# The spectrum of step one stored with the frequency outside: another word order between two stages of a long convolution

## The chip, the cores and the metric

The kernel runs on one core of a Trainium2 chip. The metric is the device time of one execution in microseconds (us). Of the core's engines, TensorE multiplies matrices out of the on-chip memory SBUF into the accumulator memory PSUM, ScalarE and VectorE work on both memories, GpSimd works on SBUF, and SyncE here only issues the transfers. Each engine takes its instructions in program order and waits for the others through semaphores.

## What is computed

The input x has 2048 tokens by 640 channels. A first block gates x with a long convolution, a second one mixes the tokens with an MLP. Shift, scale and gate of both come from c and w_mod.

```python
def _A_ref(q, k, v, shift_k, ssm_k, ssm_D):
    ...                                    # k_shift: causal convolution of k with 4 taps
    kv = k_shift * v
    kv_f = rfft(kv padded to 4096 tokens)
    kf_f = rfft(ssm_k padded to 4096)
    y = irfft(kv_f * kf_f)[:2048] + kv * ssm_D
    return q * y

def _B_ref(x, w1, b1, w2, b2):
    h = _layernorm(x)
    u = _gelu(einsum("bsd,sf->bdf", h, w1) + b1)
    return transpose(einsum("bdf,fs->bds", u, w2) + b2)

h = _layernorm(x) * (1 + ca) + sa
x = x + ga * _A_ref(h, A_k, A_v, A_shift_k, A_ssm_k, A_ssm_D)
h = _layernorm(x) * (1 + cb) + sb
x = x + gb * _B_ref(h, B_w1, B_b1, B_w2, B_b2)
```

The change lies in the Fourier transform of kv and of the convolution kernel (`ssm_k`). The names of the transforms are shortened here; the lines are otherwise those of the reference.

## The kernel before

The 640 channels are taken in five passes of 128 channels (`c` = 0 to 4, loop at line 510); a pass holds its channels as two halves of 64, one on the SBUF partitions 0 to 63 and one on 64 to 127. The 2048 tokens are split into 64 by 32, and the transform is done in two steps of matrix products.

**Step one** (`step1(side, t)`, line 210) is the transform over the 64. `side` 0 is the data kv (tile `x`, named X), `side` 1 the convolution kernel (tile `p`, named KSP), and `t` takes 8 of the 32 channels of each half. For each such channel `a` one operand column block is the stationary operand (64 columns; from X it steps by 32 words, from KSP it is unbroken), and the constant F1 (128 columns: half `h`, then frequency `k1`) is the moving one. Real and imaginary part (`ri`) go to the partitions 0 to 63 and 64 to 127 of one PSUM tile of 1024 words. Then ScalarE copies the tile into `T_z` (view `Z`, line 220). Eight such tiles fill the 8192 words of `T_z` for a pass.

**Step two** (`f2(g)`, line 224) is the transform over the 32, for 8 frequencies `k1` at a time. For each `k1`, part `ri` and half `h` there is one matmul: the stationary operand is a constant of 64 columns (`W2`), the moving operand 64 words of `T_z`, namely both sides and the 32 channels of half `h` at frequency `k1`. So it needs all eight tiles of step one. ScalarE then copies the kernel's spectrum out (`kt`, line 238), VectorE multiplies (tile `p`), and GpSimd, for the last block VectorE, adds the products into `Y`.

**The way back** is `i2` (line 255), whose result goes to the second half of `T_z` as `T2` (line 271), and `i1` (line 273); `gate` and `spill` finish a pass.

The order is written out by hand (`manual_schedule`). After f2 of a pass come step one's tiles 0 and 1 of the next pass's data, ScalarE's permutation of the next kernel (`perm`, line 164), `i2` and `i1` with data tiles 2 and 3 in between, and the four kernel-side tiles. Of these, tile 0 has its matmuls ahead of the second half of `i1` and its copy after it (`later=True`, run as `k0()`), because the copy overwrites T2. In pass 0 the order differs: step one stands at the start (lines 486 and 491), the four data tiles of pass 1 come straight after f2, and the four kernel tiles after `i1`. PSUM has three tiles in a ring for all of these and a fourth of its own. VectorE runs the products of kv (`kv_ops`) for a later pass between its f2 instructions. The modulation (`mod_load`, `mod_part`, line 342) runs within pass 0. After the five passes comes the token MLP (lines 432, 951 and 1026).

Of the kernel before, what the change touches and what calls it, by code (L numbers as in the profile page):

```python
# [11 lines left out]
AF = mybir.ActivationFunctionType  # L12
# [37 lines left out]
def mixer_kernel(ctx: ExitStack, tc: tile.TileContext, q, k, v, shift_k, ssm_k, ssm_D, w1, b1, w2, b2, c,  # L50
# [7 lines left out]
    act, dve, pool, pe, sync = nc.scalar, nc.vector, nc.gpsimd, nc.tensor, nc.sync  # L58
# [3 lines left out]
    def mem(tag, n, name=None):  # L62

        return sb.tile([128, n], F32, name=name or tag, tag=tag, bufs=1)
# [4 lines left out]
    def psum(slot=None):  # L69

        uid[0] += 1
        slot = ring[uid[0] % len(ring)] if slot is None else slot
        return psp.tile([128, 1024], F32, name=f"pst_{uid[0]}", tag=f"pst{slot}", bufs=1)
# [6 lines left out]
    T_z, T_y, T_v1 = mem("z", 8192), mem("y", 4096), mem("v", 4520)  # L80
# [11 lines left out]
    KT = [T_kt[:, 512 * i:512 * i + 512] for i in range(2)]  # L92
    TV = T_kt[:, 1024:1536].rearrange("p (n i) -> p n i", i=64)

    Z = T_z.rearrange("p (s t a k e) -> p s t a k e", s=2, t=4, a=8, e=2)
    T2 = T_z[:, 4096:8192].rearrange("p (a m e) -> p a m e", a=32, e=2)
    Y = T_y.rearrange("p (r i k) -> p r i k", r=2, i=32)
    W2 = [t.rearrange("p (k m) -> p k m", m=64) for t in T_w2]
# [111 lines left out]
    def step1(side, t, later=False):  # L210

        ps = psum()
        for a in range(8):
            i = 8 * t + a
            lhs = KSP[:, i] if side else X.rearrange("p (m i) -> p i m", i=32)[:, i]
            o = 512 * (a % 2) + 128 * (a // 2)
            for ri in range(2):
                pe.matmul(ps[64 * ri:64 * ri + 64, o:o + 128], lhs, F1[:, 128 * ri:128 * ri + 128], start=True,  # L218
                          stop=True)
        evac = lambda: act.activation(Z[:, side, t].rearrange("p a k e -> p e a k"),  # L220
                                      ps.rearrange("p (e a k) -> p e a k", a=8, e=2), AF.Copy)
        return evac if later else evac()

    def f2(g):

        ps = psum()
        for kk in range(8):
            k1 = 8 * g + kk
            for ri in range(2):
                for h in range(2):  # L230
                    o = 128 * kk + 64 * ri
                    rhs = bass.AP(tensor=T_z.tensor, offset=T_z.offset + 128 * h + 2 * k1,
                                  ap=[T_z.ap[0], [256, 32], [1, 2]])
                    pe.matmul(ps[64 * h:64 * h + 64, o:o + 64], W2[k1 // 32][:, 2 * (k1 % 32) + ri], rhs, start=True, stop=True)  # L234
        pv = ps.rearrange("p (m s i) -> p m s i", s=2, i=32)
        xs_ = pv[:, :, 0]
        kt = KT[g % 2]
        act.activation(kt.rearrange("p (m i) -> p m i", i=32), pv[:, :, 1], AF.Copy)  # L238
        pa, pb = P[:, 1024 * (g % 2):1024 * (g % 2) + 512], P[:, 1024 * (g % 2) + 512:1024 * (g % 2) + 1024]
        m16 = lambda t: t.rearrange("p (m i) -> p m i", i=32)  # L240

        def mul():
            TT(dve, m16(pa), xs_, m16(kt), ALU.mult)
            sw = bass.AP(tensor=kt.tensor, offset=kt.offset + 32, ap=[kt.ap[0], [64, 8], [-32, 2], [1, 32]])
            TT(dve, pb.rearrange("p (k r i) -> p k r i", k=8, r=2), xs_.rearrange("p (k r) i -> p k r i", r=2), sw,
               ALU.mult)

        def add(eng=pool):
            for ri, t, op in ((0, pa, ALU.subtract), (1, pb, ALU.add)):
                t = t.rearrange("p (k r i) -> p r i k", k=8, r=2)  # L250
                TT(eng, Y[:, ri, :, 8 * g:8 * g + 8], t[:, 0], t[:, 1], op)
        return mul, add
# [20 lines left out]
    def i1(half, slot=None):  # L273

        ps = psum(slot)
        for jj in range(8):
            for ri in range(2):
                for e in range(2):
                    p = slice(64 * e, 64 * e + 64)
                    for b in range(2):  # L280
                        n2 = 16 * b + 8 * half + jj
                        pe.matmul(ps[64 * b:64 * b + 64, 512 * e + 64 * jj:512 * e + 64 * jj + 64],  # L282
                                  V1[p, ri, n2], T2[p, :, 32 * ri + n2], start=ri == 0, stop=ri == 1)
        return ps
# [200 lines left out]
    for t in range(4):  # L485
        step1(0, t)
# [3 lines left out]
    for t in range(4):  # L490
        step1(1, t)
# [18 lines left out]
    for c in range(NC):  # L510
# [36 lines left out]
        if c == 0:  # L547
            mod_load(0, 4, P[:, 0:1920])
            for t in range(4):
                step1(0, t)  # L550
            ps = psum()
# [45 lines left out]
        else:  # L597
# [6 lines left out]
            t = mem("in", 4288, "wb3")  # L604
# [4 lines left out]
        if c:  # L609
            dv(7 if cn is not None else 8)  # L610
            i2(0)
            if cn is None:
                mod_part(tap, 3, pl[3])
                i2(1, dve)
                t = mem("y", 4096, "wb2")
# [19 lines left out]
        for half in range(2):  # L635
            ps = i1(half)
# [122 lines left out]
    ps = i1(1, s1)  # L759
# [121 lines left out]
    for f_ in range(4, NF):  # L881
        ps = psum().rearrange("p (h m) -> p h m", h=2)
# [202 lines left out]
```

## Time and profile before

| | |
|---|---|
| median of 3 runs | 722.91 us |
| lowest and highest | 722.14 and 728.45 us |
| span of the profiled execution | 727.4 us |
| TensorE matmul busy | 656.2 us (90%) |
| TensorE weight load busy | 632.1 us (87%) |
| VectorE busy | 492.5 us (68%) |
| ScalarE busy | 297.3 us (41%) |
| GpSimd busy | 155.7 us (21%) |

The span runs from the first to the last instruction of one execution that was recorded with a profile; the profiled execution's time is given by this span alone. In the profile's rows PE is TensorE's matmul and PEld its weight load, DVE is VectorE, ACT ScalarE, POOL GpSimd, SP SyncE; a q behind the name is the engine's instruction queue. A row of the groups gives line, engine, operation, what is written and what is read, the shapes and the count; then the busy time of the group and the mean of one in ns; then the idle time of the engine ahead of it and what ended that. A row of one tile's answer gives the shortest, median and longest duration. A row of the timeline gives start and duration in us, the same names, the count of instructions merged into it, and in brackets the idle time before it and what ended it. A row of the chain of waits gives start, duration and what the end of the program was waiting for at that time. A row of the windows gives the stretch, its length, the busy time of the chosen engine, the granted TensorE clock as a share of full speed, the transfers' share and their GB/s.

Line 59 is a helper for two-operand operations of VectorE and GpSimd, so its rows are told apart by their tiles. The program's fp32 matmul is recorded as two weight loads and two matmuls.

### The profile page before, as it was taken

How to read it: one execution, taken by the hardware profiler on the slowest of the kernel's cores; microseconds unless marked ns; L12 is line 12 of the kernel's file. 1: busy time of each engine (PE TensorE's matmuls, PEld its weight loads, DVE VectorE, ACT ScalarE, POOL GpSimd, SP SyncE). 2: the span in 40 equal slices, each digit the busy share in tenths (PEclk: the TensorE clock that was granted, in tenths of full speed). 3: DMA queues.
4: the chain of work that ended last, by engine and by line, in shares of the span. 5: the costliest groups of instructions: out<-in, count | busy, mean ns of one | idle time of the engine just before them, and what ended most of it. 6: DMA issues, size and time to landing. Idle time of an engine off the chain costs nothing.

```text
span 727.4 us, 20779 instructions
## 1 busy us (share of the span) xinstructions
PE 656.2 (90%) x9131; PEld 632.1 (87%) x9131; DVE 492.5 (68%) x861; ACT 297.3 (41%) x465; POOL 155.7 (21%) x135
## 2 busy tenths in 40 slices
PE   0798868989999989987899999999999989999997
PEld 0798558988989989777799999999999989999997
DVE  7768458958879738678895312311299868888887
ACT  0533464535645645344776312311335222333222
POOL 5197029714725428100000000000000000000000
PEclk9999989989999999679999999999999999999999
DMA  9978988427243522333022353344163333455510
GB/s 184 242 223 221 388 147 169 112 45 166 45 80 87 169 54 69 110 88 88 10 50 58 62 113 60 59 93 81 50 188 102 116 104 117 149 156 174 150 53 37
DMA packets 167184, 84.90 MB, mean 117 GB/s; under 512 B 89235, under 2 KB 157622, under 8 KB 167094
## 3 DMA queue, kind: packets, MB, share of 16 engines
q1 hardware_dynamic: 162546, 82.27, 44.8%
q10 hardware_dynamic: 4548, 1.31, 1.0%
q8 instruction: 71, 1.16, 0.7%
q14 instruction: 19, 0.16, 0.1%
HBM read 73.07 MB, written 10.49 MB: 115 GB/s over the span
## 4 chain that ended last, share of the span: by engine, by line
PE 44%; DVE 24%; POOL 8%; SPq 7%; issue 6%; ACT 6%; DMA 5%; ACTq 0%; DVEq 0%; POOLq 0%
PE pst L432 21%; PE pst L1026 7%; POOL y L59 6%; PE pst L263 5%; DVE m_w L59 4%; PE pst L218 3%; SPq L495 3%; PE pst L282 3%; DVE m_x L59 3%; DVE tap L59 3%; PE pst L234 2%; ACT m_w L939 2%; DVE kt L59 2%; PE pst L951 2%; DMA in<-in_A_k_dram 2%
## 5 line engine op out<-in xcount | busy, mean ns | idle before, releaser
L234 PEld LDWEIGHTS pst<-z,w 128*64 128x64 f32 x2560 | 94.7, 141 | 7.7 <-ACT z L220 7.3
L234 PE MATMUL pst<-z,w 128*64 128x64 f32 x2560 | 95.7, 240 | 6.2 <-ACT z L220 6.1
L59 POOL TENSOR_TENSOR y<-p 128x256 f32<-128x256 f32 x72 | 92.2, 1340 | 22.3 <-DVE p L59 21.9
L59 DVE TENSOR_TENSOR p<-pst,kt 128x512 f32<-128x512 f32 x80 | 52.9, 689 | 24.8 <-ACT kt L238 14.3
L218 PE MATMUL pst<-v,x 128*64 128x128 f32 x640 | 46.3, 306 | 25.9 <-DVE x L59 25.9
L218 PEld LDWEIGHTS pst<-v,x 128*64 128x64 f32 x640 | 44.3, 221 | 26.5 <-POOL t L457 23.6
L220 ACT ACTIVATE z<-pst 128x1024 f32<-128x1024 f32 x40 | 45.8, 1146 | 52.1 <-PE pst L218 31.7
L263 PEld LDWEIGHTS pst<-v,y 32*128 32x128 f32 x1280 | 43.3, 210 | 6.7 <-POOL y L59 3.2
L263 PE MATMUL pst<-v,y 32*128 32x64 f32 x1280 | 45.4, 297 | 3.0 <-DVE y L59 2.1
L238 ACT ACTIVATE kt<-pst 128x512 f32<-128x512 f32 x40 | 25.1, 629 | 52.5 <-PE pst L234 30.2
L830 ACT ACTIVATE pst<-pst,sm 128x640 f32<-128x640 f32 x14 | 10.7, 767 | 85.9 <-PE pst L432 85.9
L951 PE MATMUL pst<-r_z,m_w 128*128 128x320 f32 x222 | 43.1, 313 | 3.0 <-DVE m_w L59 2.5
L218 PE MATMUL pst<-v,p 128*64 128x128 f32 x640 | 39.1, 281 | 4.8 <-DVE aux L59 3.2
L218 PEld LDWEIGHTS pst<-v,p 128*64 128x64 f32 x640 | 36.6, 141 | 6.0 <-DVE aux L59 3.5
L939 ACT ACTIVATE m_w<-m_v 128x896 fp32r<-128x896 f32 x24 | 22.1, 949 | 42.7 <-DVE m_v L59 31.0
L951 PEld LDWEIGHTS pst<-r_z,m_w 128*128 128x128 f32 x222 | 34.8, 188 | 5.0 <-DVE m_w L59 4.0
L59 DVE TENSOR_TENSOR tap<-tap,kt 128x512 f32<-128x512 f32 x51 | 35.6, 697 | 1.3
L59 DVE TENSOR_TENSOR kt<-in,tap 128x512 f32<-128x512 f32 x51 | 35.0, 686 | 1.4
L271 ACT ACTIVATE z<-pst 128x512 f32<-128x512 f32 x38 | 21.2, 656 | 29.9 <-PE pst L263 29.9
L59 DVE TENSOR_TENSOR m_w<-m_v,m_w 128x896 fp32r<-128x896 f32 x24 | 26.0, 1087 | 10.5 <-ACT m_w L939 10.5
L282 PEld LDWEIGHTS pst<-z,v 64*64 64x64 f32 x1280 | 25.5, 161 | 8.6 <-issue 5.0
L282 PE MATMUL pst<-z,v 64*64 64x64 f32 x1280 | 27.5, 248 | 5.9 <-issue 3.5
(277 smaller groups left out, 1417.6 us busy)
## 6 DMA issues: line engine op xcount, KB each, us to landing
x<-in_B_w_dram SPq DMA_DIRECT2D x22, 512.0 KB
m_v<-in_B_w_dram SPq DMA_DIRECT2D x15, 384.0 KB
x<-in_B_w_dram SPq DMA_DIRECT2D x14, 384.0 KB
aux<-in_A_ssm_k_dram SPq DMA_DIRECT2D x10, 512.0 KB
in<-in_A_k_dram SPq DMA_DIRECT2D x36, 128.0 KB
in<-in_A_v_dram SPq DMA_DIRECT2D x36, 128.0 KB
m_x<-xs SPq DMA_DIRECT2D x28, 160.0 KB
out_dram<-m_x SPq DMA_DIRECT2D x28, 160.0 KB
```

The costliest lines, as they stand in the source:

```text
L59: TT = lambda eng, o, a, b, op: eng.tensor_tensor(o, a, b, op=op)
L218: pe.matmul(ps[64 * ri:64 * ri + 64, o:o + 128], lhs, F1[:, 128 * ri:128 * ri + 128], start=True, stop=True)
L220: evac = lambda: act.activation(Z[:, side, t].rearrange("p a k e -> p e a k"), ps.rearrange("p (e a k) -> p e a k", a=8, e=2), AF.Copy)
L234: pe.matmul(ps[64 * h:64 * h + 64, o:o + 64], W2[k1 // 32][:, 2 * (k1 % 32) + ri], rhs, start=True, stop=True)
L238: act.activation(kt.rearrange("p (m i) -> p m i", i=32), pv[:, :, 1], AF.Copy)
L263: pe.matmul(pp[qd // 2][:, o:o + 64], Y[p, ri, i:i + 2].rearrange("p i k -> p (i k)"), V2[p, 64 * ri:64 * ri + 64], start=ri == 0, stop=ri ...
L282: pe.matmul(ps[64 * b:64 * b + 64, 512 * e + 64 * jj:512 * e + 64 * jj + 64], V1[p, ri, n2], T2[p, :, 32 * ri + n2], start=ri == 0, stop=r ...
L432: pe.matmul(ps[0:m, h, 0:320], w_.bitcast(F32R), r_[:, 320 * h:320 * h + 320].bitcast(F32R), start=first and i == 0, stop=last and i == 2)
L495: sync.dma_start(XH[j // 8][64 * b:64 * b + 64, j % 8], dram(q, (16 * b + j) * D, [[32 * D, 64], [1, D]]))
L939: act.activation(W[n][0].bitcast(F32R), a(w_), AF.Copy)
L951: pe.matmul(bank[n], w[:, i].bitcast(F32R), r.bitcast(F32R), start=i == 0 and k == 0, stop=i == 6 and k == 2)
L1026: pe.matmul(acc[s][:, h, 0:320], w[:, f_].bitcast(F32R), u[r + h].bitcast(F32R), start=f_ == 0 and k == 0, stop=f_ == NF - 1 and k == 2)
```

## The change

`T_z` gets another order of words. Before, word 4096 s + 1024 t + 256 (a//2) + 128 h + 2 k1 + (a mod 2) held side s, tile t, channel a of the tile, half h and frequency k1; two neighbouring channels lay next to each other. Now it is word 4096 s + 2048 h + 32 k1 + 8 t + a: the frequency is outside, and the 32 channels of a half lie in a row.

```diff
-    Z = T_z.rearrange("p (s t a k e) -> p s t a k e", s=2, t=4, a=8, e=2)
+    Z = T_z.rearrange("p (s h k t a) -> p s t a h k", s=2, h=2, t=4, a=8)
...
-            o = 512 * (a % 2) + 128 * (a // 2)
+            o = 128 * a
...
-        evac = lambda: act.activation(Z[:, side, t].rearrange("p a k e -> p e a k"),
-                                      ps.rearrange("p (e a k) -> p e a k", a=8, e=2), AF.Copy)
+        evac = lambda: act.activation(Z[:, side, t], ps.rearrange("p (a h k) -> p a h k", a=8, h=2), AF.Copy)
...
-                    rhs = bass.AP(tensor=T_z.tensor, offset=T_z.offset + 128 * h + 2 * k1,
-                                  ap=[T_z.ap[0], [256, 32], [1, 2]])
+                    rhs = bass.AP(tensor=T_z.tensor, offset=T_z.offset + 2048 * h + 32 * k1,
+                                  ap=[T_z.ap[0], [4096, 2], [1, 32]])
```

Three things follow. The place of a channel's block in the PSUM tile is now in the order of the channels, where even channels used to go to the tile's first bank and odd ones to its second. ScalarE's copy reads PSUM in one row as before, and its successive words, which went 2 words apart in `T_z`, go 32 words apart. The moving operand of f2, which was 32 runs of 2 words with a step of 256, is 2 runs of 32 words with a step of 4096. The count of instructions, the values, their order within an operand and every transfer stay the same.

## The prediction, written before the changed kernel was run

> **What bounds the kernel now.** I read the page first, then the chain of waits, then the groups by line with shapes kept apart, then the timeline at the ends of the five convolution passes (c = 0 to 4, one per 128 channels).
>
> ```profile
> span 727.4 us, 20779 instructions
> ```
>
> The span is 727.4 us; the three runs lie at 722.14, 722.91 and 728.45, so the profiled execution was a long one, 4.5 us over the median and close under the highest. Terms are taken from this execution, and their sum is added to the median. The change touches lines 218, 220 and 234 only, all within the first 294 us. After that comes the token MLP, which takes any delay over unchanged.
>
> ```profile
> 181.99 10.21 POOL y L59 x8
> ...
> 195.38 3.58 PE pst L263 x120
> ...
> 271.57 17.86 PE pst L234 x475
> ```
>
> In the chain of waits step two (f2, line 234) has the chain on TensorE only in the last pass. In c = 2 the chain runs on GpSimd's additions into Y, eight in a row at 1.28 us each, and TensorE's f2 lies beside them. So a faster f2 is worth little there, while a later start of f2 starts the additions later.
>
> ```profile
> L234 PE MATMUL pst<-z,w 128*64 128x64 f32 x2560 | 95.7, 240 | 6.2 <-ACT z L220 6.1
> L220 ACT ACTIVATE z<-pst 128x1024 f32<-128x1024 f32 x40 | 45.8, 1146 | 52.1 <-PE pst L218 31.7 <-PE pst L282 20.2
> L218 PE MATMUL pst<-v,x 128*64 128x128 f32 x640 | 46.3, 306 | 25.9 <-DVE x L59 25.9
> L218 PEld LDWEIGHTS pst<-v,x 128*64 128x64 f32 x640 | 44.3, 221 | 26.5 <-POOL t L457 23.6
> L218 PE MATMUL pst<-v,p 128*64 128x128 f32 x640 | 39.1, 281 | 4.8 <-DVE aux L59 3.2
> L218 PEld LDWEIGHTS pst<-v,p 128*64 128x64 f32 x640 | 36.6, 141 | 6.0 <-DVE aux L59 3.5
> ```
>
> Each program matmul shows as two passes. Line 220 is the evacuation of step one: 40 of 1.146 us, and f2's 6.1 us of waiting are for it, 1.2 ahead of each pass. A tile of step one is 32 passes: 46.3/640 × 32 = 2.3 us on the data side (x), 39.1/640 × 32 = 1.96 us on the kernel side (p). ScalarE at 1.15 us per tile keeps up today.
>
> **Part 1: what f2 gains.** The 2560 passes read 64 words as two runs of 32 instead of 32 runs of 2. One pass takes 95.7/2560 = 37.4 ns with 64 moving columns; a pass of step one (p), whose moving operand F1 is one run of 128 words, takes 39.1/640 = 61.1 ns. If nothing but the columns counted, f2 could not fall under half of that, 30.5 ns, so the gain lies between 0 and 6.9 ns. But a pass also has its weight load and start, which do not halve with the columns: if these are only 14 ns of the 61.1, the 37.4 are explained without any cost of the short runs (14 + 47/2). Below nothing (a loss) is excluded, since the longer run asks no more of the read. I take 0. Even the upper end is small in the time: in c = 1 to 4 only the first block of 64 passes stands before GpSimd's additions, 64 × 6.9 ns = 0.44 us each, and at the end of c = 4 about 1 us more, 2.8 us in all. What hides the rest is GpSimd's gapless run of additions; without it up to 17.6 us (2560 × 6.9 ns) would show.
>
> **Part 2: what the evacuation costs.** The read from PSUM is one row of 1024 words before and after. The write changes: successive words went 2 words apart, now 32 words (128 bytes) apart. No ScalarE write in this trace steps that far, so I bound it.
>
> ```profile
> L421 ACT ACTIVATE wb0b<-x 128x1024 fp32r<-128x1024 f32 x10 | 10.0, 1051 | 2.2 <-PE pst L432 2.2
> L408 ACT ACTIVATE wb<-x 128x512 fp32r<-128x512 f32 x8 | 4.5, 620 | 0.0
> L170 ACT ACTIVATE tap<-rows 128x256 f32<-128x256 f32 x3 | 2.0, 680 | 0.0
> ...
> L59 DVE TENSOR_TENSOR m_x<-m_x 128x320 f32<-128x320 f32 x35 | 17.2, 492 | 1.2
> L59 DVE TENSOR_TENSOR m_w<-m_v,m_w 128x896 fp32r<-128x896 f32 x24 | 26.0, 1087 | 10.5 <-ACT m_w L939 10.5
> ```
>
> ScalarE on unbroken runs takes 1051 ns for 1024 and 620 for 512: 0.84 ns per element and 190 ns fixed. So 1051 ns is the floor, 0.1 us below today. Line 170 reads with a step of 4 words: 680 ns where 190 + 256 × 0.84 = 405 would do, 1.07 ns more per element. A read by TensorE with exactly the new step of 32 words stands above: the stationary load from x takes 221 ns, the unbroken one from p 141, for 64 columns 1.25 ns more each.
>
> ```profile
> L59 DVE TENSOR_TENSOR y<-p x8: 597/1204/1515, 138.7 to 294.0; 128x256 f32<-128x256 f32 x8
> ```
>
> VectorE's additions into Y read both inputs with a step of 64 words. Its unbroken slope is (1087 − 492)/576 = 1.03 ns, so 256 elements would take 426 ns; the fastest took 597 (0.67 ns more per element), the median 1204 (3.04 for two streams, 1.52 for one, part of it perhaps GpSimd in the way). So the ends are 0 and 1.52 ns: an evacuation E of 1.05 to 2.61 us. I take the middle of the two nearest rows, ScalarE's own (1.07) and the one with the same step (1.25): 1.16 × 1024 + 1051 = 2.24 us, 1.09 more than now.
>
> [...]
>
> **Part 3: how E comes to the path.** The ScalarE queue is in order: behind these evacuations stand those of the inverse steps (line 271), the permutation of the next kernel spectrum (164) and f2's copies (238). f2 needs all eight tiles of a pass.
>
> ```profile
> 265.06 1.17 ACT L220 ACTIVATE z<-pst 128x1024 f32<-128x1024 f32 x1 [6.09 <-PE pst L282]
> ...
> 270.45 1.07 ACT L220 ACTIVATE z<-pst 128x1024 f32<-128x1024 f32 x1 [0.59 <-PE pst L218]
> 274.92 1.29 DVE L59 TENSOR_TENSOR p<-pst,kt 128x512 f32<-128x512 f32 x2 [5.02 <-ACT kt L238]
> ...
> 275.69 17.91 POOL L59 TENSOR_TENSOR y<-p 128x256 f32<-128x256 f32 x14 [6.95 <-DVE p L59]
> ```
>
> c = 4: four kernel-side evacuations run from 265.06 to 271.52, 6.46 us; each waits about 0.6 us for TensorE. At E = 2.24 they run back to back. Neighbours on ScalarE overlap by about 0.1 us (line 421's ten of 1.051 us, issued in pairs, kept it busy for 10.0), so 4E − 0.3 = 8.66, 2.2 us later. VectorE has waited 5 us for f2, and GpSimd's 14 additions run gapless behind it: **2.2 us**, all of it.
>
> ```profile
> 164.69 1.18 ACT L220 ACTIVATE z<-pst 128x1024 f32<-128x1024 f32 x1 [7.55 <-PE pst L282]
> ...
> 170.06 1.09 ACT L220 ACTIVATE z<-pst 128x1024 f32<-128x1024 f32 x1 [0.61 <-PE pst L218]
> ...
> 173.84 0.62 ACT L238 ACTIVATE kt<-pst 128x512 f32<-128x512 f32 x1 [2.70 <-PE pst L234]
> ...
> 175.09 1.28 DVE L59 TENSOR_TENSOR p<-pst,kt 128x512 f32<-128x512 f32 x2
> ```
>
> c = 2: again 6.46 us, so 2.2 later. Here VectorE is busy with the next block's products until 175.09, 0.63 us after f2's copy is ready (174.46): **1.6 us** reach GpSimd.
>
> ```profile
> 215.09 1.20 ACT L220 ACTIVATE z<-pst 128x1024 f32<-128x1024 f32 x1 [6.51 <-PE pst L282]
> ...
> 220.47 1.08 ACT L220 ACTIVATE z<-pst 128x1024 f32<-128x1024 f32 x1 [0.62 <-PE pst L218]
> ...
> 225.52 1.28 DVE L59 TENSOR_TENSOR p<-pst,kt 128x512 f32<-128x512 f32 x2
> ```
>
> c = 3: 6.46 us once more, VectorE busy as before: **1.6 us**.
>
> ```profile
> 113.35 1.14 ACT L220 ACTIVATE z<-pst 128x1024 f32<-128x1024 f32 x1 [5.61 <-PE pst L218]
> 115.10 1.10 ACT L220 ACTIVATE z<-pst 128x1024 f32<-128x1024 f32 x1 [0.61 <-PE pst L218]
> 119.53 1.29 DVE L59 TENSOR_TENSOR p<-pst,kt 128x512 f32<-128x512 f32 x2 [1.89 <-ACT kt L238]
> 121.15 5.91 POOL L59 TENSOR_TENSOR y<-p 128x256 f32<-128x256 f32 x4
> ```
>
> c = 1: only the last two tiles are close: 2E − 0.1 = 4.38 against 2.85 (113.35 to 116.20), 1.5 later. The first addition has 0.3 us to spare (120.82 to 121.15), the following products none: **1.4 us**.
>
> ```profile
> 27.32 1.16 ACT L220 ACTIVATE z<-pst 128x1024 f32<-128x1024 f32 x1 [2.68 <-PE pst L218]
> 40.52 1.08 ACT L220 ACTIVATE z<-pst 128x1024 f32<-128x1024 f32 x1 [0.59 <-PE pst L218]
> 44.95 1.29 DVE L59 TENSOR_TENSOR p<-pst,kt 128x512 f32<-128x512 f32 x2 [4.17 <-ACT kt L238]
> 48.26 19.76 POOL L59 TENSOR_TENSOR y<-p 128x256 f32<-128x256 f32 x16
> 63.02 8.38 PE L218 MATMUL pst<-v,x 128*64 128x128 f32 x128 [2.29 <-DVE x L59]
> 81.82 1.99 PE L342 MATMUL tap<-aux,sm 128*32 128x320 f32 x12 [2.37 <-DMA aux<-in_w_mod_dram]
> ```
>
> c = 0: eight tiles, 14.28 us (27.32 to 41.60) against 8E − 0.7 = 17.2, 2.9 later. GpSimd has 2.0 us to spare (46.24 to 48.26) and TensorE 2.29 before the next step one; the 0.6 to 0.9 left and the longer last evacuation (1.1) run into the 2.37 us that TensorE waits for the modulation weights: **0**. If E were 2.61 that cover is gone and 3.2 us show (5.9 − 2.3 + 1.5 + 0.5 − 2.37).
>
> The data-side tiles of c = 1 to 4 come every 2.3 us from TensorE, more than E − 0.1; the first two of each pass and the permutation behind them lie beside the inverse step's first matmuls (3.58 us in c = 2, and its wait for Y before that): 0, and nothing but the next evacuation would wait if that cover were gone.
>
> Sum: 0 + 1.4 + 1.6 + 1.6 + 2.2 = 6.8 us.
>
> ```profile
> 102.83 3.79 PE L218 MATMUL pst<-v,p 128*64 128x128 f32 x64
> ...
> 109.82 5.22 PE L218 MATMUL pst<-v,p 128*64 128x128 f32 x64 [3.21 <-DVE aux L59]
> ...
> 109.80:112.40 2.60, 2.58 (x24) 0.50 0.63 154
> ```
>
> TensorE's wait ahead of f2 grows from 1.2 to some 3.4 us. After 3.21 us of idling at 109.82 the granted clock was 0.50, and the same 64 passes took 5.22 instead of 3.79 us. That could come in c = 2, 3 and 4, so 0 to 4.3 us; I take one, 1.4. [...] Forecast: 722.9 + 6.8 + 1.4 = 731.1 us.
>
> The other edits: the tile's eight blocks now fill one PSUM bank after the other instead of taking turns. f2 itself writes sixteen blocks in a row into one bank at 37 ns a pass, so 0. No transfer, wait or instruction is added, and SP's and GpSimd's queues are not touched.
>
> **Rivals.** *Not slower: ScalarE's writes are buffered and the step costs nothing.* Then E is 1.05, f2 starts 0.1 us earlier, and with whatever Part 1 gives the time is 720 to 723. For it: the rows that show a price are reads. Against: VectorE and ScalarE and the weight load all pay. It decides below E = 1.75, where ScalarE still keeps up (only the last tile's 0.6 us shows, less VectorE's slack). *The dear step:* E = 2.61, as one stream of the median 1204 ns gives. Then 3.2 + (5.12 − 2.85 − 0.1) + 2 × (4 × 2.61 − 0.3 − 6.46 − 0.63) + 3.68 = 3.2 + 2.2 + 6.1 + 3.7 = 15.2 us, with three slow clocks 19.5: 738 to 742. [...] *The change does not reach f2:* the pairs are already read at full rate; this is my value for Part 1, and against it stands only the bound.
>
> **How the numbers follow.** Chances: forecast (E from 1.75 to 2.4, 724 to 734) 0.56; free write 0.22; dear step 0.22. The range leaves out some 0.1 at each end: 721 to 745. One per cent, about what a measurement of this kernel tells from no change, is 7.2 us, so slower means above 730.1: the dear step and 0.6 of the forecast, 0.22 + 0.33 = 0.55. Faster by that much would need 7 us where Part 1 has at most 2.8: 0.03. Within: 0.42.
>
> **What would show it.** Line 220's mean tells E at once: near 2.2 here, near 1.05 or 2.6 in the rivals. Line 234's busy time should stay at 95.7 us; under 85 my Part 1 is wrong. The four kernel-side evacuations before f2 should stand without gaps and f2 start about 2 us later against them, GpSimd's additions gapless as before. If line 220 is at 2.2 and the time has not moved, the slack of Part 3 is misread; if line 238 or 271 grows too, the cost is not in the write pattern.

## The result, and the profile after

Over 20 runs of each, the median is 720.34 us with the change and 723.16 us without it; the ratio is 0.9936 with a 95% interval of 0.9912 to 0.9961, so 4.6 us faster (2.8 to 6.4). The ratio, like those of the experiments, leaves out runs in the chip's slower state, here three of the 20 with the change (726.5 to 728.8 us); over all 20 of each the medians differ by 2.8 us and the means by 3.6. The forecast was 731.1 us, and the sign was wrong. The profiled execution took 724.0 us, with a span of 721.9; it and the one before were both longer than their medians, so the two spans are not set against each other, only their rows.

These are rows of the page of the changed kernel. Line 233 is step two (234 before), line 237 its copy of the spectrum (238 before).

```profile
L233 PE MATMUL pst<-z,w 128*64 128x64 f32 x2560 | 80.9, 227 | 15.0 <-ACT z L220 10.7
L220 ACT ACTIVATE z<-pst 128x1024 f32<-128x1024 f32 x40 | 76.3, 1966 | 31.0 <-PE pst L218 30.2
L59 POOL TENSOR_TENSOR y<-p 128x256 f32<-128x256 f32 x72 | 79.6, 1141 | 30.8 <-DVE p L59 30.5
L237 ACT ACTIVATE kt<-pst 128x512 f32<-128x512 f32 x40 | 23.9, 598 | 43.6 <-PE pst L233 27.7
```

Four things moved. A matmul pass of step two fell from 37.4 to 80.9/2560 = 31.6 ns on average. ScalarE's copy of step one grew from 1.146 to 1.966 us. GpSimd's additions into Y, which no line of the change touches, fell from 92.2 to 79.6 us of busy time, the mean of one from 1340 to 1141 ns. And line 220 no longer waits for the inverse step: 20.2 us of its idle time ended with line 282 before, none of it with line 281 now. The row of the additions before:

```profile
L59 POOL TENSOR_TENSOR y<-p 128x256 f32<-128x256 f32 x72 | 92.2, 1340 | 22.3 <-DVE p L59 21.9
```

The timeline of c = 3: the start of step two, the first copy of the kernel's spectrum and GpSimd's additions, first before, then after:

```profile
221.61 19.01 PE L234 MATMUL pst<-z,w 128*64 128x64 f32 x511 [1.24 <-ACT z L220]
...
224.25 0.62 ACT L238 ACTIVATE kt<-pst 128x512 f32<-128x512 f32 x1 [2.70 <-PE pst L234]
...
226.28 5.05 POOL L59 TENSOR_TENSOR y<-p 128x256 f32<-128x256 f32 x4 [7.49 <-DVE p L59]
231.27 1.01 POOL L59 TENSOR_TENSOR aux<-aux,rows 1x64 f32<-1x64 f32 x2
232.35 12.80 POOL L59 TENSOR_TENSOR y<-p 128x256 f32<-128x256 f32 x10
```

```profile
224.86 15.14 PE L233 MATMUL pst<-z,w 128*64 128x64 f32 x511 [2.14 <-ACT z L220]
...
227.00 0.60 ACT L237 ACTIVATE kt<-pst 128x512 f32<-128x512 f32 x1 [2.19 <-PE pst L233]
...
228.61 2.18 POOL L59 TENSOR_TENSOR y<-p 128x256 f32<-128x256 f32 x2 [7.47 <-DVE p L59]
231.14 2.20 POOL L59 TENSOR_TENSOR y<-p 128x256 f32<-128x256 f32 x2 [0.35 <-DVE p L59]
233.29 0.78 POOL L59 TENSOR_TENSOR aux<-aux,rows 1x64 f32<-1x64 f32 x2
234.16 11.23 POOL L59 TENSOR_TENSOR y<-p 128x256 f32<-128x256 f32 x10
```

From the first addition to the last it took 18.87 us before (226.28 to 245.15) and takes 16.78 now (228.61 to 245.39), although GpSimd now waits for VectorE in between. Step two starts at 221.61 before and 224.86 after; the kernel's spectrum is first copied at 224.25 and at 227.00. So the stretch from the start of step two to the last addition fell from 23.54 to 20.53 us: 2.1 of it on GpSimd's additions, 0.5 in TensorE's first block (2.64 to 2.14 up to the copy), 0.4 between that copy and the first addition (2.03 to 1.61).

Against this stands a later start of step two. The end of c = 3 after the change, the place that the prediction showed of before:

```profile
264.20 2.37 PE L281 MATMUL pst<-z,v 64*64 64x64 f32 x128
264.38 1.96 ACT L220 ACTIVATE z<-pst 128x1024 f32<-128x1024 f32 x1 [3.98 <-PE pst L218]
...
266.50 5.46 PE L218 MATMUL pst<-v,p 128*64 128x128 f32 x96
...
268.51 5.45 ACT L220 ACTIVATE z<-pst 128x1024 f32<-128x1024 f32 x3 [2.17 <-PE pst L218]
...
274.01 11.45 PE L233 MATMUL pst<-z,w 128*64 128x64 f32 x384 [2.05 <-ACT z L220]
```

The first kernel-side copy now runs at 264.38, beside the second half of the inverse step (264.20 to 266.57); before, it began after it. The reason is in the new order of words: tile t fills the words 8t to 8t + 7 of every 32, and the second half of `i1` reads the words 16 to 31 of every 32 of T2, so tile 0 overwrites nothing that is still to be read, and the wait fell away. Only three copies are left between the kernel-side matmuls and step two, and these stand back to back. Step two starts 7.51 us after those matmuls began (266.50 to 274.01), against 6.69 before (264.88, the row below, to the 271.57 of the chain of waits): 0.8 us later.

```profile
264.88 5.46 PE L218 MATMUL pst<-v,p 128*64 128x128 f32 x96
```

The waits of the whole run agree: step two waited 6.1 us for line 220 before, 10.7 now, 0.9 more in each of five passes.

So c = 3, which GpSimd bounds, gains 3.0 us up to the last addition. Not all of it reaches the next pass: from the start of step two in c = 3 to that in c = 4 it took 49.96 us before and takes 49.15 now, only 0.8 less. Of the other 2.2 us, 0.8 is the later start, and 0.9 is idle time of TensorE in the inverse step, for which the profile shows no wait (`issue` in these rows, before and after); the remaining 0.5 came earlier in the inverse step and was not followed.

```profile
260.43 0.33 PE L282 MATMUL pst<-z,v 64*64 64x64 f32 x4 [0.67 <-issue]
```

```profile
262.04 0.33 PE L281 MATMUL pst<-z,v 64*64 64x64 f32 x4 [1.58 <-issue]
```

In c = 2 the same 3.0 us are gained (the inverse step's block of 120 passes began 24.18 us after step two before, and 21.17 after), and the pass went from 50.41 to 50.03 us. There the clock took the gain: from 196.00 to 201.76 the granted TensorE clock was 0.59, against 1.00 for the same block before. These rows of the chain of waits after the change show two blocks at the low clock, in c = 2 (line 262) and c = 1 (line 233), each with its like at full clock:

```profile
121.82 3.61 PE pst L233 x64
...
196.00 5.76 PE pst L262 x120
...
246.01 3.58 PE pst L262 x120
...
274.01 2.11 PE pst L233 x64
```

So the two profiled executions show what became faster and what became slower, but not in which passes the 4.6 us of the timed runs arise.

### The profile page after: what moved, and what is told of

Same layout as the page of the kernel before. It is cut to its first block, busy times and chain, and to the rows that moved or that the text cites. A ratio compares the mean times of both kernels' runs of the same rounds, so it can differ in the third digit from the quotient of the medians.

```text
span 721.9 us, 20770 instructions
## 1 busy us (share of the span) xinstructions
PE 641.2 (89%) x9131; PEld 617.0 (85%) x9131; DVE 491.8 (68%) x861; ACT 326.0 (45%) x465; POOL 142.4 (20%) x135
## 3 DMA queue, kind: packets, MB, share of 16 engines
q8 instruction: 71, 1.16, 0.7%
## 4 chain that ended last, share of the span: by engine, by line
PE 41%; DVE 29%; DMA 8%; ACT 7%; issue 5%; SPq 5%; POOL 4%; ACTq 0%; DVEq 0%; POOLq 0%
PE pst L431 21%; PE pst L1025 7%; PE pst L262 4%; DVE m_w L59 4%; PE pst L218 4%; POOL y L59 3%; SPq L494 3%; DVE p L59 3%; DVE m_x L59 3%; DVE tap L59 3%; DVE kt L59 2%; PE pst L281 2%; DMA aux<-in_A_ssm_k_dram 2%; ACT m_w L938 2%; PE pst L950 2%
## 5 line engine op out<-in xcount | busy, mean ns | idle before, releaser
L233 PE MATMUL pst<-z,w 128*64 128x64 f32 x2560 | 80.9, 227 | 15.0 <-ACT z L220 10.7
L233 PEld LDWEIGHTS pst<-z,w 128*64 128x64 f32 x2560 | 79.1, 142 | 16.2 <-ACT z L220 11.9
L220 ACT ACTIVATE z<-pst 128x1024 f32<-128x1024 f32 x40 | 76.3, 1966 | 31.0 <-PE pst L218 30.2
L59 POOL TENSOR_TENSOR y<-p 128x256 f32<-128x256 f32 x72 | 79.6, 1141 | 30.8 <-DVE p L59 30.5
L218 PE MATMUL pst<-v,x 128*64 128x128 f32 x640 | 45.9, 303 | 25.0 <-DVE x L59 24.3
L218 PEld LDWEIGHTS pst<-v,x 128*64 128x64 f32 x640 | 43.8, 221 | 26.8 <-POOL t L456 23.3
L829 ACT ACTIVATE pst<-pst,sm 128x640 f32<-128x640 f32 x14 | 10.7, 767 | 86.1 <-PE pst L431 86.1
L262 PEld LDWEIGHTS pst<-v,y 32*128 32x128 f32 x1280 | 40.4, 196 | 6.9 <-POOL y L59 2.9
L262 PE MATMUL pst<-v,y 32*128 32x64 f32 x1280 | 42.3, 282 | 4.0 <-DVE y L59 2.4
L218 PE MATMUL pst<-v,p 128*64 128x128 f32 x640 | 39.4, 284 | 6.0 <-DVE aux L59 4.6
L938 ACT ACTIVATE m_w<-m_p 128x896 fp32r<-128x896 f32 x12 | 11.4, 952 | 46.8 <-DVE m_p L59 40.6
L281 PEld LDWEIGHTS pst<-z,v 64*64 64x64 f32 x1280 | 24.2, 154 | 9.1 <-issue 5.5
```

Of the source, the lines that this page charges most:

```text
L59: TT = lambda eng, o, a, b, op: eng.tensor_tensor(o, a, b, op=op)
L220: evac = lambda: act.activation(Z[:, side, t], ps.rearrange("p (a h k) -> p a h k", a=8, h=2), AF.Copy)
L262: pe.matmul(pp[qd // 2][:, o:o + 64], Y[p, ri, i:i + 2].rearrange("p i k -> p (i k)"), V2[p, 64 * ri:64 * ri + 64], start=ri == 0, stop=ri ...
L938: act.activation(W[n][0].bitcast(F32R), a(w_), AF.Copy)
```

## The experiments

All times are against the kernel before, run on the same chip in the same series; intervals are 95%. A time without an interval is that of a single run. Where a diff has only lines with a plus, the lines of the kernel before that they replace are left out.

### The write alone and the read alone

The write alone is the kernel before with the new order in the copy; the rest, step two's operand too, is the old one:

```diff
-    Z = T_z.rearrange("p (s t a k e) -> p s t a k e", s=2, t=4, a=8, e=2)
+    Z = T_z.rearrange("p (s h k t a) -> p s t a h k", s=2, h=2, t=4, a=8)
...
-        evac = lambda: act.activation(Z[:, side, t].rearrange("p a k e -> p e a k"),
-                                      ps.rearrange("p (e a k) -> p e a k", a=8, e=2), AF.Copy)
+        evac = lambda: act.activation(Z[:, side, t], ps.rearrange("p (a h k) -> p a h k", a=8, h=2), AF.Copy)
```

> The spectrum is written in the new order but step two reads the old addresses, so its operands hold other words. Theory A (step two's short-run reads are what slowed both TensorE and GpSimd; the write only costs ScalarE time): line 220 near 1.97 us, a pass of step two near 37.4 ns, GpSimd's additions into Y near 1.34 us as before; each pass starts step two about 0.9 us later, so 3 to 5 us slower than before (ratio 1.004 to 1.007). Theory B (GpSimd became faster through the other timing that the slower copy brings, not through the reads): additions near 1.14 us here too, and the time about as before.

The read alone is the kernel before with the new operand. In both, step two's operands hold other words.

```diff
-                    rhs = bass.AP(tensor=T_z.tensor, offset=T_z.offset + 128 * h + 2 * k1,
-                                  ap=[T_z.ap[0], [256, 32], [1, 2]])
+                    rhs = bass.AP(tensor=T_z.tensor, offset=T_z.offset + 2048 * h + 32 * k1,
+                                  ap=[T_z.ap[0], [4096, 2], [1, 32]])
```

> The spectrum is written in the old order and step two reads the new addresses, so its operands hold other words. Theory A: line 220 stays at 1.15 us, a pass of step two takes 29 to 31.6 ns, GpSimd's additions 1.14 us; 8 to 11 us faster than before (ratio 0.985 to 0.989), more than the whole change. Theory B: pass near 30 ns, but additions still 1.34 us, so only the first block of each pass shows: 1 to 3 us faster (ratio 0.996 to 0.999).

The write alone gave a ratio of 0.9977 (0.9945 to 1.0009), the read alone 0.9894 (0.9842 to 0.9946). Rows of the groups, write alone and then read alone:

```profile
L233 PE MATMUL pst<-z,w 128*64 128x64 f32 x2560 | 96.0, 240 | 0.5 <-DVE p L59 0.2
L59 POOL TENSOR_TENSOR y<-p 128x256 f32<-128x256 f32 x72 | 89.9, 1320 | 20.7 <-DVE p L59 20.5
L220 ACT ACTIVATE z<-pst 128x1024 f32<-128x1024 f32 x40 | 76.6, 1973 | 34.0 <-PE pst L218 33.3
```

```profile
L234 PE MATMUL pst<-z,w 128*64 128x64 f32 x2560 | 79.3, 223 | 10.1 <-DVE p L59 7.6 <-issue 1.2 <-ACT aux L289 1.2
L59 POOL TENSOR_TENSOR y<-p 128x256 f32<-128x256 f32 x72 | 79.1, 1131 | 22.7 <-DVE p L59 22.5
```

The slow copy leaves passes and additions as they were (96.0 us, 1320 ns); the new read alone brings both down (79.3 us, 1131 ns). That is theory A. But the time of the write alone missed what A expected, and the rows say why: step two was idle for 0.5 us and never waited for line 220. With the write in one order and the read in the other, step two's first blocks read words of some tiles only, so they could start before the last copy; the read alone lost its wait in the same way. Both times are flattered, and both runs were made again with the waits kept.

### The same two with the waits of the kernel before

The write steps by 32 words within each tile's own 1024 words; the read takes runs of 32 words from the end of each side backwards, so that the first block needs the last tile. In both, step two's operands hold other words.

```diff
+    zt = T_z[:, 4096 * side + 1024 * t:4096 * side + 1024 * t + 1024]
+    evac = lambda: act.activation(zt.rearrange("p (x y) -> p y x", y=32),
+                                  ps.rearrange("p (y x) -> p y x", y=32), AF.Copy)
```

> The kernel before, but ScalarE's copy writes each tile's own 1024 words in another order, successive words 32 apart, so that the words land in other places and all waits stay those of the kernel before. Theory A (the step costs ScalarE about 0.8 us a copy, and this comes to the path ahead of step two): line 220 near 1.97 us, passes 37.4 ns and additions 1.34 us as before, step two waits longer for line 220, and the time is 3 to 5 us above before (ratio 1.004 to 1.007). Rival (the slow copy is hidden whatever the waits are, and the first write-only run was right): line 220 near 1.97, ratio 0.997 to 1.001.

```diff
+                    rhs = bass.AP(tensor=T_z.tensor, offset=T_z.offset + 2048 * (1 - h) + 32 * (63 - k1),
+                                  ap=[T_z.ap[0], [4096, 2], [1, 32]])
```

> The kernel before, but step two reads runs of 32 words, from the end of each side backwards, so that its first block waits for the last tile as before; the operands hold other words. Theory A: line 220 at 1.15 us, step two waits some 6 us for it as before, passes 31 ns, additions 1.13 us; the time lies 1 to 4 us over the first read-only run, which did not wait, at a ratio of 0.985 to 0.993 to before. Rival (most of the first read-only run's gain was the wait that it lost): ratio 0.995 to 1.0.

The stepped write is slower, 1.0117 (1.0080 to 1.0154), 8.5 us; the long read is faster, 0.9894 (0.9842 to 0.9946), as without the wait. Rows of the groups and of the timeline at the end of c = 3 for the stepped write:

```profile
L235 PE MATMUL pst<-z,w 128*64 128x64 f32 x2560 | 99.8, 247 | 10.8 <-ACT z L221 10.7
L221 ACT ACTIVATE z<-pst 128x1024 f32<-128x1024 f32 x40 | 78.9, 2036 | 30.2 <-PE pst L218 15.5 <-PE pst L283 14.3
```

```profile
273.20 1.97 PE L218 MATMUL pst<-v,p 128*64 128x128 f32 x32
...
273.38 3.90 ACT L221 ACTIVATE z<-pst 128x1024 f32<-128x1024 f32 x2 [4.15 <-PE pst L283]
...
277.53 3.63 ACT L221 ACTIVATE z<-pst 128x1024 f32<-128x1024 f32 x2 [0.26 <-PE pst L218]
281.21 8.99 PE L235 MATMUL pst<-z,w 128*64 128x64 f32 x209 [2.04 <-ACT z L221]
```

Here the first copy waits for the inverse step as before (4.15 us, ended by line 283), and four copies stand ahead of step two: 8.01 us from 273.20 to 281.21, against 6.69 before and 7.51 in the changed kernel. This is the case that the prediction worked out. The time is twice what was expected of this run from the changed kernel's rows, and slower passes are part of the reason: after waits of 2.0 to 2.1 us for line 221 (1.2 for line 220 before) step two took 1.0 to 1.1 us longer in each of c = 1 to 3 (20.1 us from 227.12 to 247.24 in c = 3, against 19.1 from 221.61 to 240.68 before), and it was busy for 99.8 us in the whole run, 4.1 more than before. From 40 to 300 us the granted clock was 0.91 on average, against 0.96 before. How much of the 4.1 reaches the time, behind GpSimd, was not measured. Rows of the long read:

```profile
L234 PE MATMUL pst<-z,w 128*64 128x64 f32 x2560 | 79.3, 223 | 12.0 <-ACT z L220 6.1 <-DVE p L59 3.1 <-issue 2.6
L59 POOL TENSOR_TENSOR y<-p 128x256 f32<-128x256 f32 x72 | 78.8, 1124 | 26.9 <-DVE p L59 26.7
```

Step two waits its 6.1 us for line 220 again, and passes and additions are fast: the gain is the read's. In this trace c = 2 takes 46.7 us and c = 3 47.8 from one start of step two to the next, 3.7 and 2.1 less than before.

### Short runs, or the step between them

Only the moving operand of step two is changed; its words are others. In the order of the blocks: pairs 1000 bytes apart, runs of 4 words 2048 bytes apart, pairs 512 bytes apart.

```diff
+                    rhs = bass.AP(tensor=T_z.tensor, offset=T_z.offset + 128 * h + 2 * k1,
+                                  ap=[T_z.ap[0], [250, 32], [1, 2]])
```

```diff
+                    rhs = bass.AP(tensor=T_z.tensor, offset=T_z.offset + 128 * h + 2 * k1,
+                                  ap=[T_z.ap[0], [512, 16], [1, 4]])
```

```diff
+                    rhs = bass.AP(tensor=T_z.tensor, offset=T_z.offset + 4096 + 64 * h + 2 * (k1 % 32),
+                                  ap=[T_z.ap[0], [128, 32], [1, 2]])
```

> Step two reads 32 runs of 2 words as before, with a step of 250 words (1000 bytes) in place of 256 (1024 bytes); the operands hold other words. If the short runs are what costs, passes stay at 37 ns and the additions at 1.3 us. If it is the step of a power of two (all runs in the same place of the memory), passes fall to 31 ns and the additions to 1.13 us.

> Step two reads 16 runs of 4 words with a step of 512 words; the operands hold other words. If each run has a price, half the runs cost half: passes near 34 ns, additions near 1.23 us. If a run of 4 words (16 bytes) already reads at full rate, passes at 31 ns and additions at 1.13 us. If the step of a power of two costs, 37 ns and 1.34 us as before.

> Step two reads 32 runs of 2 words with a step of 128 words (512 bytes), all from the half of the spectrum that is written last; the operands hold other words. If any step that is a power of two costs, passes stay at 37 ns and additions at 1.3 us. If it takes 1024 bytes to meet the same place, passes fall to 31 ns and additions to 1.15 us.

> Timed repeat of the pairs with a step of 250 words. Theory (the step of 1024 bytes costs, not the short run): ratio to before 0.985 to 0.992, as with the long runs under the same waits (0.9894). Rival (its one look was a lucky run): 0.995 to 1.0.

Rows of the groups, in the order pairs at 1000 bytes, runs of 4 at 2048, pairs at 512:

```profile
L59 POOL TENSOR_TENSOR y<-p 128x256 f32<-128x256 f32 x72 | 80.7, 1159 | 23.4 <-DVE p L59 23.0
L234 PE MATMUL pst<-z,w 128*64 128x64 f32 x2560 | 78.7, 220 | 10.3 <-ACT z L220 6.1 <-issue 2.1 <-DVE p L59 2.0
```

```profile
L234 PE MATMUL pst<-z,w 128*64 128x64 f32 x2560 | 81.7, 225 | 10.0 <-ACT z L220 6.1 <-issue 2.1 <-DVE p L59 1.6
L59 POOL TENSOR_TENSOR y<-p 128x256 f32<-128x256 f32 x72 | 80.5, 1154 | 24.7 <-DVE p L59 24.1
```

```profile
L234 PE MATMUL pst<-z,w 128*64 128x64 f32 x2560 | 95.6, 240 | 6.3 <-ACT z L220 6.1 <-DVE p L59 0.2
L59 POOL TENSOR_TENSOR y<-p 128x256 f32<-128x256 f32 x72 | 91.7, 1334 | 22.2 <-DVE p L59 21.9
```

Pairs 1000 bytes apart read as fast as runs of 32 words (78.7 us, additions 1159 ns); pairs 512 bytes apart cost as much as at 1024 (95.6 us, 1334 ns). The run is 2 words at 1000, 512 and 1024 bytes, so a short run alone is not the cause. The step matters, with pairs: the two powers of two tried are slow, and 1000 bytes, the only other step tried, is not; with 4 words at a stop 2048 bytes cost next to nothing (81.7 us). Timed, the pairs at 1000 bytes gave 0.9868 (0.9801 to 0.9935), no smaller a gain than the long runs. A single run of each took 715.0 us (pairs at 1000), 711.2 (runs of 4) and 725.2 (pairs at 512), with a median of 724 to 725 for the kernel before. Why these steps are slow was not measured.

### What slows GpSimd, and which engine carries the gain

The additions read both inputs in one row instead of stepping by 64 words, so they add other products.

```diff
-                t = t.rearrange("p (k r i) -> p r i k", k=8, r=2)
+                t = t.rearrange("p (r i k) -> p r i k", k=8, r=2)
```

> The kernel before, but the additions into Y read both inputs in one row of 256 words instead of stepping by 64 words; they add other products. If GpSimd is slowed because its own stepped reads meet step two's reads in the same places, the additions take 0.85 to 0.95 us, as unbroken reads on GpSimd would, and stay there while step two runs. If step two's reads slow anything that GpSimd reads, they lie 0.15 to 0.25 us above that, 1.05 us or more. Passes of step two 37 ns in both.

> The kernel before, with the additions into Y reading in one row (other products are added), timed. If GpSimd's additions are what the passes of c = 1 to 3 wait for, taking them from 1.34 to 0.76 us with step two's pass left at 37 ns gives at least what the changed reads gave: ratio 0.985 to 0.99. If TensorE's passes carry the gain, it stays at 0.995 to 1.0.

Together with the long read from the end:

> Both: additions in one row and step two's long runs read from the end, waits as before. With the additions at 0.76 us GpSimd no longer limits, so a pass of 31 in place of 37 ns now shows in every block of step two: 2 to 3 us in each of five passes, ratio 0.96 to 0.975. If something else has become the bound (VectorE's products, ScalarE's copies), it is no better than the additions alone, within 0.004.

Rows of the additions, from the groups of both timed runs, and, from the answers for GpSimd's `y` (shortest, median and longest), their spread in the kernel before and in the first of the two:

```profile
L59 POOL TENSOR_TENSOR y<-p 128x256 f32<-128x256 f32 x72 | 53.2, 764 | 46.6 <-DVE p L59 46.5
```

```profile
L59 POOL TENSOR_TENSOR y<-p x72: 1071/1368/1827, 48.3 to 292.5; 128x256 f32<-128x256 f32 x72
```

```profile
L59 POOL TENSOR_TENSOR y<-p x72: 728/765/817, 48.6 to 285.7; 128x256 f32<-128x256 f32 x72
```

```profile
L59 POOL TENSOR_TENSOR y<-p 128x256 f32<-128x256 f32 x72 | 51.0, 736 | 38.2 <-DVE p L59 38.0
```

In a row the additions take 764 ns beside the old reads of step two and 736 beside the new ones: 0.03 us between them, where stepping additions lose 0.2. So GpSimd is slowed, from 1141 to 1340 ns, when its own reads step by 256 bytes and TensorE's by 1024 at the same time. The trace of the kernel before bears out the "at the same time": its 49 additions that ran wholly beside step two have a median of 1439 ns, the 18 that ran wholly outside it one of 1149; in the changed kernel the two medians are 1114 and 1160. The 764 ns lie below both values that were expected of additions in a row.

The time: 716.0 us in a single run; timed, the additions alone 0.9916 (0.9880 to 0.9952), both changes 0.9808 (0.9751 to 0.9865). Taking work from GpSimd alone is worth 6 us, though TensorE's pass is still 37 ns, so GpSimd was the bound, as the chain of waits said. But 0.9916 falls between the two expectations, and the trace says why: TensorE is close behind. From the start of step two to the inverse step's block of 120 passes it took 24.2 us in c = 2 and 3 before, and 23.3 with the additions in a row; TensorE has no idle time left there (line 263 waits 0.6 us in the whole run, against 3.0 before). The change reached 21.2 because it made both faster, the additions and TensorE's passes. Faster additions alone stop at 23.3; faster passes alone were not run, but GpSimd's gapless additions would still take their 18.9 us.

The faster read adds some 1.1% on top of additions in a row, as much as it gained with stepping ones (0.9894). That is less than expected for a TensorE-bound step two and more than nothing, so it falls between both expectations.

### The price of the write

```diff
+    zt = T_z[:, 4096 * side + 1024 * t:4096 * side + 1024 * t + 1023]
+    evac = lambda: act.activation(zt.rearrange("p (x y) -> p y x", y=33),
+                                  ps[:, 0:1023].rearrange("p (y x) -> p y x", y=33), AF.Copy)
...
+    dve.memset(T_z.rearrange("p (b x) -> p b x", x=1024)[:, :, 1023:1024], 0.0)
```

> The kernel before, but ScalarE's copy writes with a step of 33 words (31 in a row, 33 rows; one word of each tile is set to zero at the start instead). If a single word per step is the cost, whatever the step, line 220 stays at 1.97 to 2.05 us as with 32 words. If the cost of 32 words was the power of two, it falls to 1.0 to 1.7 us. Passes 37 ns and additions 1.34 us in both.

```profile
L221 ACT ACTIVATE z<-pst 128x1023 f32<-128x1023 f32 x40 | 80.1, 2091 | 28.8 <-PE pst L283 14.9 <-PE pst L218 13.8
```

With 33 words it costs 2091 ns, no less than with 32 (2036), where single words 2 apart cost 1146 before: on the write it is not the power of two that costs. A single run took 731.1 us.

### Versions with the long read and a cheap write

All three versions here are edits of the changed kernel. In the first, ScalarE walks in the order of `T_z` and steps in PSUM; in the second, the matmuls of step one write PSUM in steps of 4 and 8 words, and ScalarE reads it in a row.

```diff
-        evac = lambda: act.activation(Z[:, side, t], ps.rearrange("p (a h k) -> p a h k", a=8, h=2), AF.Copy)
+        evac = lambda: act.activation(Z[:, side, t].rearrange("p a h k -> p h k a"),
+                                      ps.rearrange("p (a h k) -> p h k a", a=8, h=2), AF.Copy)
```

> The changed kernel, with ScalarE's copy walking in the order of the target: it writes runs of 8 words and reads PSUM with a step of 128 words. If a step costs ScalarE the same on a PSUM read as on an SBUF write, line 220 stays near 2 us and the time is that of the changed kernel (ratio 0.994). If PSUM reads may step freely, line 220 falls to 1.05 to 1.15 us and the time is that of theory A for the reads alone (ratio 0.985 to 0.989). Under theory B the latter would be no faster than the changed kernel.

```diff
+    Z = T_z.rearrange("p (s m t b a) -> p s t b m a", s=2, m=128, t=4, b=2)
...
+            pv = ps[:, 512 * (a // 4):512 * (a // 4) + 512].rearrange("p (k h c) -> p h k c", h=2, c=4)[:, :, :, a % 4]
...
+                pe.matmul(pv[64 * ri:64 * ri + 64], lhs, F1[:, 128 * ri:128 * ri + 128], start=True, stop=True)
...
+        evac = lambda: act.activation(Z[:, side, t], ps.rearrange("p (b m a) -> p b m a", b=2, m=128), AF.Copy)
...
+                    rhs = bass.AP(tensor=T_z.tensor, offset=T_z.offset + 64 * k1 + 32 * h,
+                                  ap=[T_z.ap[0], [4096, 2], [1, 32]])
```

> Step one's matmuls write PSUM with a step of 4 or 8 words, so that ScalarE reads PSUM in one row and writes runs of 4 words; the half is inside the frequency. If TensorE writes PSUM with a step at no cost, a pass of step one stays at 61 (kernel side) and 72 ns (data side), line 220 falls to 1.05 to 1.15 us, and the time is that of theory A for the reads alone (ratio 0.985 to 0.989). If the stepped write holds TensorE, step one's passes grow to 100 ns or more, 1280 of them by 30 ns or more each, and the time is 5 us or more above the changed kernel.

Rows of the groups of the first, then of the second:

```profile
L59 POOL TENSOR_TENSOR y<-p 128x256 f32<-128x256 f32 x72 | 79.0, 1136 | 26.9 <-DVE p L59 26.7
L220 ACT ACTIVATE z<-pst 128x1024 f32<-128x1024 f32 x40 | 40.8, 1023 | 56.3 <-PE pst L218 56.1
```

```profile
L218 PE MATMUL pst<-v,x 128*64 128x128 f32 x640 | 46.0, 305 | 26.8 <-DVE x L59 26.4 <-DVE p L59 0.4
L220 ACT ACTIVATE z<-pst 128x1024 f32<-128x1024 f32 x40 | 40.9, 1023 | 56.5 <-PE pst L218 56.1
L218 PE MATMUL pst<-v,p 128*64 128x128 f32 x640 | 40.5, 286 | 6.4 <-DVE aux L59 4.6 <-ACT p L164 1.1 <-issue 0.8
```

The copy takes 1023 ns in both, less than in the kernel before. Stepping by 128 words in PSUM costs ScalarE nothing here, and TensorE's stepped write shows no price (40.5 us for the kernel side, as in the long read, whose step one writes PSUM as before). The ratios are 0.9879 (0.9838 to 0.9920) and 0.9895 (0.9847 to 0.9943). Against the changed kernel's 0.9936 (0.9912 to 0.9961) the first would be worth another 0.6%, what the change's own write gives away; but the intervals overlap a little and come from two series, so the times alone do not show it.

The last version adds GpSimd's walk along i, which reads runs of 32 words and writes Y with a step of 64:

```diff
-                TT(eng, Y[:, ri, :, 8 * g:8 * g + 8], t[:, 0], t[:, 1], op)
+                t = t.rearrange("p (k r i) -> p r k i", k=8, r=2)
+                TT(eng, Y[:, ri, :, 8 * g:8 * g + 8].rearrange("p i k -> p k i"), t[:, 0], t[:, 1], op)
```

> The version whose copy writes runs of 8 words, with the additions walking along i instead of along k: they read runs of 32 words and write Y with a step of 64 words; the values are the reference's. If GpSimd pays for stepped reads alone, the additions fall to 0.8 us and the ratio to 0.97 to 0.98. If a stepped write costs it as much as two stepped reads, they stay at 1.1 us or more, and the ratio at 0.988.

```profile
L234 PE MATMUL pst<-z,w 128*64 128x64 f32 x2560 | 78.8, 223 | 10.8 <-ACT z L220 5.6 <-issue 2.5 <-DVE p L59 2.4
L59 POOL TENSOR_TENSOR y<-p 128x256 f32<-128x256 f32 x72 | 51.2, 744 | 38.5 <-DVE p L59 38.2
```

GpSimd writes with a step of 64 words at no visible price (744 ns, against 736 with reads in a row and writes in runs of 8 words). The median of four runs is 708.73 us, the ratio 0.9829 (0.9758 to 0.9901): the fastest kernel of this study that computes the reference, if not quite the 0.97 to 0.98 expected.

## Why the prediction was wrong, step by step

**What bounds the kernel** was read rightly: GpSimd's additions in c = 2 and 3. The run with faster additions alone bears it out, and shows that TensorE was only 0.8 us behind in such a pass.

**Part 1, the step that failed first.** The gain of a pass was bounded at 0 to 6.9 ns and put at 0; it is 5.8 (37.4 to 31.6), and line 234's 95.7 us became 80.9, under the 85 that the prediction named as the sign. The argument was that 14 ns for load and start explain 37.4 without any price of the read. That a number can be explained without a cost is no sign that the cost is absent, and nothing excluded the upper end. The long read under the old waits gained 7.7 us (0.9894), where the prediction allowed 2.8 at most. TensorE's moving operand has such a price here: with pairs 512 or 1024 bytes apart a pass takes 37 ns, with pairs 1000 bytes apart 31.

**The cover was taken as fixed: the error that turned the sign.** "What hides the rest is GpSimd's gapless run of additions" supposed that these do not change. They became 0.2 us shorter each, because the old reads had slowed them, and 14 of them stand in a row in a pass. Less the time that GpSimd now waits for VectorE, that is 2.1 us of the 3.0 gained up to the last addition in c = 3. No rival had this.

**Part 2** had the mechanism and overrated the size: E is 1.97 us, not 2.24; the step costs (1966 − 1051)/1024 = 0.89 ns per element, not 1.16. The read row nearest in kind, ScalarE's 1.07, was the better of the two.

**Part 3.** "The four kernel-side evacuations before f2 should stand without gaps", 2.2 us, failed: three do, since the new order freed the first one of its wait for the inverse step, and step two starts 0.8 to 0.9 us later. The text took every wait as kept ("no transfer, wait or instruction is added") and did not ask whether one is taken away. Where that wait stays, the stepped write under the old waits cost 8.5 us (5.8 to 11.2), near the sum of 8.2, but the agreement is partly luck. The delay of the four copies came as worked out, only smaller: with the measured 2.04 us, 4E − 0.3 − 6.46 is 1.4 us, and 1.3 was measured (8.01 against 6.69), so by the same formulas the 6.8 us of the sum would be some 3.9. In the stepped write's profiled execution step two was busy for 4.1 us more than before, where the sum had one slow clock of 1.4.

**The slow clock** of 1.4 us was expected after the longer wait in one of c = 2, 3 and 4. In the profiled execution it came in none of them (granted 1.00 at the start of step two; in c = 4 384 passes took 11.45 us, 29.8 ns each). It came in c = 1, after a wait of 2.03 us: granted 0.53 from 121.82 to 125.43, and 3.61 us for 64 passes that took 2.11 in c = 4, so 1.5 us on the chain of waits. It came in c = 0 as well (0.66 from 42.22 to 46.00). Size and kind were right, the place was not; no run shows what sets the place, and one execution can't say how often it comes. The term for c = 0 can't be told from the changes of the transfers there.

**The other edits** were put at 0, rightly as far as the rows go: with the blocks in their new places in PSUM, line 218 was busy for 45.9 and 39.4 us (data and kernel side), against 46.3 and 39.1 before.

**The rival "not slower"** expected a time of 720 to 723 from a free write. The time came out so, but the write is not free (1.97 us a copy, against 1.15 before), and no run shows a buffer; that range was met by luck: the faster reads and the lost wait made up for the dear write.

## What to carry to other kernels

Before calling a gain hidden, ask whether the work that hides it uses the same memory as the work that becomes faster: here TensorE's reads slowed GpSimd, which the edit does not name, from 1141 to 1340 ns an addition, and its rows showed it by a spread (1071 to 1827 ns) that its own work does not explain. In TensorE's fp32 operands look first at two words at a stop with a step of a power of two: here 512 and 1024 bytes cost 37 ns a pass, and four words at each stop, or a step of 1000 bytes, brought it to 31 or 32. When two engines bound a stage closely, as GpSimd and TensorE do here, look for the edit that helps both. When a layout is changed, compare which tiles each instruction overlaps as well as the pattern's speed, and let ScalarE do the stepping where it reads PSUM, which cost nothing here (1023 ns a copy, against 1146 before and 1966 with the step on the write).

## What the runs showed of the hardware that was not expected

- TensorE's moving operand in fp32: runs of 2 words 512 or 1024 bytes apart 37 ns a pass, 1000 bytes apart 31 ns, runs of 4 words 2048 bytes apart 32 ns.
- The same reads slow GpSimd's additions that step by 256 bytes from 1.14 to 1.34 us, and those that read in a row by 0.03 us only (764 against 736 ns); ScalarE's copy of 512 words (line 237) went from 629 to 598 ns as well.
- ScalarE writes single words 32 or 33 words apart at 0.9 to 1.0 ns per element more, but reads PSUM with a step of 128 words, writing runs of 8, at 1023 ns for 1024 elements.
- TensorE writes PSUM in steps of 4 and 8 words at 63 ns a pass, no more than the long read's 63 with unbroken writes, and GpSimd writes with a step of 64 words at 744 ns, where two reads with that step cost 1136.
